# Delta-rule attention and two MLPs on one core: own staging tiles for two chunks, retuned planner numbers, fused masks and GpSimd copies

## The chip, the cores and the metric

The kernel runs on one core of a Trainium2 chip. The metric is the device time of one execution in microseconds, the median of several runs. The engines are named as in the profile: PE is TensorE's matmul side and PEld its weight loads, DVE is VectorE, ACT ScalarE, POOL GpSimd, SP the engine that issues every DMA of this kernel.

## What is computed

```python
def _attn_ref(q, k, v, beta):                      # q, k, v: [4, 8, 768, 48] float32
    k_n = k / (np.linalg.norm(k, axis=-1, keepdims=True) + 1e-06)
    state = np.zeros((B, H, D, D), dtype=np.float32)
    for t in range(S):
        kt, vt, bt = (k_n[:, :, t], v[:, :, t], beta[:, :, t, None])
        y[:, :, t] = np.einsum('bhd,bhde->bhe', q[:, :, t], state)
        v_old = np.einsum('bhde,bhd->bhe', state, kt)
        state = state + bt[:, :, :, None] * np.einsum('bhd,bhe->bhde', kt, vt - v_old)
    return y

# reference: attention, then x = [3072, 384], then two MLPs 384 -> 2048 -> 384
h = x @ w_in;  g = 0 if h <= -1, h if h >= 1, else (h + 1) ** 2 / 4;  x = g @ w_out
h = x @ w_in2; g = h * clip(h + 3, 0, 6) / 6;                         out = g @ w_out2
```

The weights arrive as 64-bit floating-point numbers; the kernel reads their two 32-bit words and makes from them a high and a low fp32r half.

## The kernel before

**Attention.** The 768 steps are cut into 12 chunks of 64. For all 32 heads of a chunk the kernel loads k, v and q, takes the norms of k, and forms, for each half `hb` of the heads, the products of k with k (they go to X, scaled) and of k with q (they go to KQ, and everything past the diagonal is masked to zero). `load_tok` brings the k or q of one half into one of two staging tiles, ST_78 (k) and ST_79 (q), 128x512 each; `transposes` turns the tile on PE into a bank and ACT or DVE copies the bank into KQ; `products` multiplies. Then `inverse` inverts a unit triangular matrix per head, `scale_v` scales v, `wstage` (from chunk 1 on) multiplies the inverse (in G_74 for even chunks, G_75 for odd ones) with k, and `chain` passes the state on and makes y. The y of half 1 of a chunk goes partly through a small tile YS and six DMAs into the MLP's input XB.

**Inverse.** Chunk 0 does its 16 elimination steps on DVE, small instructions of some 0.2 us that each need the one before; chunks 1 to 11 do theirs on POOL.

**MLPs.** Layer 1 takes chunk 0 as a block of 256 columns, chunk 1 as another, then pairs of chunks as blocks of 512; layer 2 takes six blocks of 512. A block goes through 16 slices f of the hidden width: H multiplies XB with WLA or WLB in three steps (high by high, low by high, high by low), ACT and DVE apply the activation and split it into GH and GL, O multiplies these with w_out. For a block of 256 columns H and O of one f are 6 passes of 3 matmuls each, 128x256. `wload` loads one f of the weights raw into one of four RAWL buffers or RAWR and converts it in two halves; each half costs ACT and DVE three or so instructions each (lines 366, 826, 828, 831, 357).

**Order.** No engine's order is written by hand. `Plan` collects the operations with their dependences and a priority; `Plan.emit` places them one by one, always the one that could start soonest by its own table of durations, ties by priority, and what it chooses becomes the in-order queue of each engine. PR holds the priorities (kv, tok, norm, pm, sv, w, chain, y, lv) and its other numbers (a bias for POOL and ACT where an operation could go to several engines, a margin for MLP work). Before the first MLP matmul, wherever PE would idle by the table, `emit` puts filler matmuls `bank_100<-GH_69`, 128x512, whose result nobody reads.

Names used below: `emit`'s filler rule (213 and 427 in its body), `cpalt` (a copy on ACT or DVE, `AD`), `ttalt` (an elementwise operation on DVE or POOL, `DP`), `masking` (the separate mask operation, L535), L506 (X out of the bank), L514 (KQ out of the bank on ACT, mask later) and L516 (the same on DVE, mask at once), L471 (transposes), L389 (all other matmuls).

## Time and profile before

| | us |
|---|---|
| median of 3 runs | 1086.45 |
| lowest and highest run | 1084.42, 1089.5 |
| the profiled execution | 1090.76 |
| its span in the trace | 1089.0 |
| busy PE / DVE / ACT / POOL | 1045.1 / 662.6 / 595.7 / 277.6 |
| first matmul of the MLPs, from the span's start | 87.06 |

The profile is one execution, so times within the span are told as microseconds from its start. PE is busy 96% of the span, but its busy time before 87.06 us holds 176 filler matmuls. The granted clock in the rows (PEclk) is 1.00 for TensorE's upper level of 2.4 GHz; in stretches with parts at 1.2 GHz the mean lies between.

### The profile page before, as it was taken

To read this page: it belongs to the slowest core of one execution; us is meant where nothing else is said; L and a number is where in the kernel's file an instruction comes from. 1 tells how busy PE (TensorE), PEld (TensorE's weight loads), DVE (VectorE), ACT (ScalarE), POOL (GpSimd) and SP (SyncE) were. 2 spreads that over 40 slices of the span, in tenths; PEclk is the share of its full clock that TensorE was granted. 3 is DMA by queue.
4 is the path that set the end of the run, shared out by engine and by line. 5 is a ranking of instruction groups with operands and counts; after the bars stand their busy time and mean duration, and the time that the engine had idled before them with its cause. 6 is when DMAs were issued, how large, how long until landed. Compare 5 with 4: busy or idle time off the path is not lost.

```text
span 1089.0 us, 25916 instructions
## 1 busy us (share of the span) xinstructions
PE 1045.1 (96%) x10684; PEld 890.1 (82%) x10684; DVE 662.6 (61%) x1258; ACT 595.7 (55%) x1164; POOL 277.6 (25%) x652
## 2 busy tenths in 40 slices
...
GB/s 179 191 142 66 61 99 66 45 63 36 59 21 97 69 17 59 90 45 46 40 57 83 80 257 139 116 1 88 1 41 47 1 87 2 59 29 1 29 1 29
DMA packets 174757, 71.86 MB, mean 66 GB/s; under 512 B 121264, under 2 KB 170544, under 8 KB 174640
## 3 DMA queue, kind: packets, MB, share of 16 engines
...
q8 instruction: 84, 1.38, 0.6%
...
## 4 chain that ended last, share of the span: by engine, by line
PE 72%; DVE 11%; ACT 5%; DMA 4%; POOL 3%; issue 3%; SPq 1%; DVEq 0%; POOLq 0%; ACTq 0%
PE bank L389 71%; DMA RAWL<-in_moe_w_in_dram 2%; DVE X L506 2%; POOL TL L571 1%; POOL TMP L566 1%; ACT KQ L514 1%; DVE GF L880 1%; PE bank L471 1%; DVE KQ L535 1%; DMA RAWR<-in_moe_w_in_dram 1%; DVE GL L357 1%; DVE DL L624 1%; ACT G L366 1%; SPq L815 1%; DVE XB L777 1%
## 5 line engine op out<-in xcount | busy, mean ns | idle before, releaser
L389 PE MATMUL bank<-XB,WLA 128*128 128x512 f32 (+1 forms) x1404 | 341.2, 386 | 13.4 <-DMA XB<-YS 7.1
L389 PEld LDWEIGHTS bank<-XB,WLA 128*128 128x128 f32 x1404 | 251.9, 193 | 62.1 <-ACT TBS L828 6.6
L357 DVE TENSOR_TENSOR GL<-GF,GH 128x512 fp32r<-128x512 f32 (+1 forms) x208 | 139.4, 671 | 82.9 <-PE bank L389 57.4
L884 DVE SCALAR_TENSOR_TENSOR GF<-GF,bank 128x512 f32<-128x512 f32 x96 | 66.1, 688 | 193.0 <-ACT GF L883 192.9
L366 ACT ACTIVATE GH<-GF 128x512 fp32r<-128x512 f32 (+1 forms) x202 | 120.9, 599 | 114.3 <-DVE GF L884 69.1
L883 ACT ACTIVATE GF<-bank 128x512 f32<-128x512 f32 x96 | 57.5, 599 | 204.5 <-PE bank L389 203.6
L566 POOL TENSOR_TENSOR TMP<-TL,DL 128x126 f32<-128x126 f32 (+25 forms) x293 | 113.0, 386 | 115.8 <-DVE DL L624 65.7
L571 POOL TENSOR_TENSOR TL<-TL,TMP 128x126 f32<-128x126 f32 (+25 forms) x293 | 126.6, 432 | 23.0
L389 PE MATMUL bank<-GH,WLA 128*128 128x512 f32 (+1 forms) x504 | 121.5, 373 | 2.6 <-DVE GH L368 1.5
L389 PE MATMUL bank<-XB,WLB 128*128 128x512 f32 (+1 forms) x468 | 112.4, 382 | 0.2 <-DVE GF L880 0.2
L389 PE MATMUL bank<-WLA,GH 128*128 128x384 f32 x576 | 112.3, 336 | 0.0
L389 PEld LDWEIGHTS bank<-WLA,GH 128*128 128x128 f32 x576 | 102.8, 188 | 6.4
L389 PEld LDWEIGHTS bank<-GH,WLA 128*128 128x128 f32 x504 | 85.9, 192 | 20.7 <-ACT GH L366 3.5
L389 PEld LDWEIGHTS bank<-XB,WLB 128*128 128x128 f32 x468 | 83.4, 191 | 15.5 <-DVE GF L880 0.4
L880 DVE SCALAR_TENSOR_TENSOR GF<-bank,GF 128x512 f32<-128x512 f32 (+1 forms) x112 | 68.6, 612 | 45.0 <-ACT GF L879 43.8
L878 ACT ACTIVATE GF<-bank 128x512 f32<-128x512 f32 (+1 forms) x112 | 59.8, 534 | 60.6 <-PE bank L389 56.1
L389 PE MATMUL bank<-GL,WLA 128*128 128x512 f32 (+1 forms) x252 | 65.9, 370 | 0.0
L879 ACT ACTIVATE GF<-GF 128x512 f32<-128x512 f32 (+1 forms) x112 | 63.5, 567 | 2.4
L389 PE MATMUL bank<-WLA,GL 128*128 128x384 f32 x288 | 61.5, 334 | 0.0
L389 PEld LDWEIGHTS bank<-WLA,GL 128*128 128x128 f32 x288 | 51.0, 188 | 0.0
L389 PE MATMUL bank<-GH 128*128 128x512 f32 x176 | 50.8, 437 | 0.0
L389 PEld LDWEIGHTS bank<-GL,WLA 128*128 128x128 f32 x252 | 43.9, 191 | 8.2 <-issue 0.3
(135 smaller groups left out, 1357.6 us busy)
## 6 DMA issues: line engine op xcount, KB each, us to landing
...
```

Source lines behind the costliest of these rows:

```text
L357: alts[e] = (d, lambda e=e: ENG[e].tensor_tensor(out=val(out), in0=val(in0), in1=val(in1), op=op))
L366: lambda: nc.scalar.activation(out=val(out), in_=val(in_), func=AF.Copy, scale=scale))
L389: nc.tensor.matmul(o, l, r, start=start, stop=stop)
L471: nc.tensor.transpose(bk.tile[0:112, p * 128:(p + 1) * 128], ST[i][:, p, 0:112], IDN)
L506: P.op("dve", 335, lambda bk=bk, u0=u0, rr=rr, ro=ro: nc.vector.tensor_tensor(out=X[rr, u0:u0 + NP, :], in0=bk.tile[ro].rearrange("p (a x) ...
L566: P.op(te, d, lambda t=t, s=s, r0=r0, a0=a0, a1=a1, m=m: ve.tensor_tensor(out=t[:, a0:a1], in0=TL[:, r0 + a0:r0 + a1, s:s + 1].to_broadcas ...
L571: P.op(te, d, lambda t=t, s=s, r0=r0, a0=a0, a1=a1: ve.tensor_tensor(out=TL[:, r0 + a0:r0 + a1, 0:s], in0=TL[:, r0 + a0:r0 + a1, 0:s], in1 ...
L878: P.op("act", da, lambda: nc.scalar.activation(out=gf, in_=ps, func=AF.Relu, scale=0.5, bias=0.5), r=[hkey(hb)], w=[gk], prio=MP)
L879: P.op("act", da + 48, lambda: nc.scalar.activation(out=gf, in_=gf, func=AF.Square), w=[gk], r=[gk], prio=MP)
L880: P.op("dve", 1.06 * n + 60, lambda: nc.vector.scalar_tensor_tensor(out=gf, in0=ps, scalar=1.0, in1=gf, op0=ALU.max, op1=ALU.min), r=[hkey ...
L883: P.op("act", da, lambda: nc.scalar.activation(out=gf, in_=ps, func=AF.Relu, scale=1.0 / 6.0, bias=0.5), r=[hkey(hb)], w=[gk], prio=MP)
L884: P.op("dve", 1.06 * n + 60, lambda: nc.vector.scalar_tensor_tensor(out=gf, in0=gf, scalar=1.0, in1=ps, op0=ALU.min, op1=ALU.mult), r=[hke ...
```

## The change

PR gets other numbers (kv, tok, norm, pm, sv, w, chain, y, lv, bias, biasa, margin) and new ones (fgap, me, c3, back, dh, and POOL in dw). Beyond that:

- **Staging.** Half 1 of chunks 0 and 1 gets staging tiles of its own: four 128x512 views of G_74 (k and q of chunk 0) and G_75 (chunk 1), zeroed by four more POOL memsets at the start. The zeroing of G itself moves behind the products of its chunk (`zero_g`).
- **Transfers.** A DMA's duration in the planner's table has other values, given per kind; DMAs marked `bulk` (v, weights, tokens and k of chunks 1 and up) are not placed further than `back` ahead of the modelled queue.
- **Masks.** ACT's evacuation of KQ is weighed with 500 more (`extra`), so that DVE's, which masks at once (L516, now L529), is chosen more often and the separate mask less.
- **Copies.** `cpalt` may use POOL for the SBUF to SBUF copies in X, LT and G (`PR["c3"]`), and POOL may do the low-half subtraction of the weights (`dw`).
- **Fillers.** They count 228 or 430 instead of 213 or 427, and must leave 150 instead of 100.
- `wload` takes a list of slices, which holds one everywhere; its views are written in three dimensions.

```diff
+PR = dict(kv=-2.522, tok=-1.749, norm=-2.601, tr=-1.803, prod=-3.087, pm=-0.932, inv=-2.162, sv=0.06, w=-1.449, chain=-0.205, y=-0.76,
+          wl=-0.036, wls=0.003, mp=0, lv=-1.0, first=3.58, bias=83.342, fill=3000, ..., biasa=652.767,
+          ..., fgap=150, me=500, c3=('act', 'dve', 'pool'), back=1500, dh=0, margin=738.749, ..., dw=('dve', 'pool'), pq=190)
...
+                    if o["bulk"]:
+                        t = max(t, dma_free - PR["back"])
...
-                        end = t + o["alts"][e][0] + bias.get(e, 0.0)
+                        ex = o["extra"]
+                        end = t + o["alts"][e][0] + bias.get(e, 0.0) + ex.get(e, 0.0)
...
-                    if x + d > t - 100.0:
+                    if x + d > t - PR["fgap"]:
...
+            if e == "pool":
+                alts[e] = (190 + 1.1 * n, lambda: nc.gpsimd.tensor_copy(val(out), val(in_)))
...
+    gs = [G[i].rearrange("p u e s -> p (u e s)") for i in range(2)]
+    extra = [gs[0][:, 0:512], gs[0][:, 512:1024], gs[1][:, 1024:1536], gs[1][:, 1536:2048]]
+    ST += [x.rearrange("p (a x) -> p a x", a=NP) for x in extra]
...
-        i = stage[0] % NST
+        if c < 2:
+            i = (0 if hb == 0 else 2 + 2 * c) + stage[0] % 2
+        else:
+            i = stage[0] % NST
...
-                                      q=qd(SH[dl], PO[g][dl], SH[dl]))
+                                      q=qd(SH[dl], PO[g][dl], SH[dl]), extra={"act": PR["me"]})
...
-            cpalt(AD, 256, X[p0:p0 + 32, us, 0:32], X[p0:p0 + 32, us, 32:64], False,
+            cpalt(PR["c3"], 256, X[p0:p0 + 32, us, 0:32], X[p0:p0 + 32, us, 32:64], False,
...
+    def zero_g(s_):
+        P.tag = ""
+        zk = [("zg", s_)] + [("gw", s_, hb, dl) for hb in range(2) for dl in range(2)] + tkeys(s_, 0) + tkeys(s_, 1) + \
+            [("st", 2 + 2 * s_ + i, b) for i in range(2) for b in range(2)]
+        zero(G[s_][32:64, :, 0, :], zk, 1200)
+        zero(G[s_][32:64, :, 1, 0:32], zk, 600)
+        zero(G[s_][96:128, :, 0, 0:32], zk, 600)
...
+    for i in range(4):
+        zero(ST[2 + i], [("st", 2 + i)] + ([("braw", 0), ("braw", 1)] if i >= 2 else []), 470)
```

What this makes of the queues, at three places. In the rows a name such as `bank_100` is a bank of PSUM, and `x25` counts equal instructions in a row; a source line is shifted by the change (L471 becomes L484, L389 becomes L396).

**1. PE and SP at the start.** PE, from the last products of half 0 of chunk 0 (`bank_97<-KQ`) to the first of half 1 (`bank_101<-KQ`), before:

```order
L389 MATMUL bank_97<-KQ 64x128 x2
L389 MATMUL bank_100<-GH_69 128x512 x25
L471 MATMUL bank_98<-IDN,ST_78 112x128 x4
L389 MATMUL bank_100<-GH_69 128x512 x3
L471 MATMUL bank_99<-IDN,ST_79 112x128 x4
L389 MATMUL bank_100<-GH_69 128x512 x6
L389 MATMUL bank_101<-KQ 64x128 x2
```

and now:

```order
L396 MATMUL bank_97<-KQ 64x128 x2
L484 MATMUL bank_98<-IDN,G_74 112x128 x4
L484 MATMUL bank_99<-IDN,G_74 112x128 x4
L396 MATMUL bank_100<-GH_69 128x512 x12
L396 MATMUL bank_101<-KQ 64x128 x2
```

34 fillers between the two products have become 12, and both transposes stand right behind the products of half 0. Ahead of the products of half 0 stood 6 fillers, the transposes of k, 2 fillers, those of q, 6 fillers; now 4, k, q, 3.

SP, from the loads of v of chunk 0 on (E_71 is v, KN_77 is k of chunk 1 in natural order, RAWL the raw weights), before:

```order
L429 DMA E_71<-in_v_dram 64x16x48 x2
L422 DMA KN_77<-in_k_dram 64x16x48 x2
L815 DMA RAWL<-in_moe_w_in_dram 48x3x256
L815 DMA RAWL<-in_moe_w_in_dram 16x3x256
L815 DMA RAWL<-in_moe_w_in_dram 48x3x256
L815 DMA RAWL<-in_moe_w_in_dram 16x3x256
L411 DMA ST_78<-in_k_dram 64x8x48 x2
L411 DMA ST_79<-in_q_dram 64x8x48 x2
L815 DMA RAWL<-in_moe_w_out_dram 128x768
```

and now:

```order
L442 DMA E_71<-in_v_dram 64x16x48
L424 DMA G_74<-in_k_dram 64x8x48 x2
L424 DMA G_74<-in_q_dram 64x8x48 x2
L442 DMA E_71<-in_v_dram 64x16x48
L435 DMA KN_77<-in_k_dram 64x16x48 x2
L424 DMA ST_78<-in_k_dram 64x8x48 x2
L424 DMA ST_79<-in_q_dram 64x8x48 x2
L424 DMA G_75<-in_k_dram 64x8x48 x2
L424 DMA G_75<-in_q_dram 64x8x48 x2
L831 DMA RAWL<-in_moe_w_in_dram 48x3x256
```

All tokens of chunks 0 and 1 now go out ahead of the first weights, half 1 of chunk 0 ahead of half of v; before, its loads waited for the staging tiles and stood behind four loads of weights.

**2. POOL beside the inverse of chunk 0**, which runs on DVE. Before, from the last zeroing of G_75 to the first work on chunk 1's inverse (TL):

```order
L399 MEMSET G_74 32x16x32
L399 MEMSET G_75 32x16x64
L399 MEMSET G_75 32x16x32 x2
L357 ISA
L357 TENSOR_TENSOR E_72<-E_72,NRM_90 64x16x48
L574 MEMSET TL 128x512
```

and now, from the zeroing of the new staging views:

```order
L409 MEMSET G_75 128x512 x2
L362 ISA
L362 TENSOR_TENSOR E_71<-E_71,NRM_89 64x16x48
L409 MEMSET G_74 32x16x64
L409 MEMSET G_74 32x16x32 x2
L409 MEMSET G_75 32x16x64
L409 MEMSET G_75 32x16x32 x2
L548 TENSOR_TENSOR KQ<-KQ,MSK 64x4x64 x2
L362 TENSOR_TENSOR E_72<-E_72,NRM_90 64x16x48
L587 MEMSET TL 128x512
```

Half of the scaling of chunk 0's v (E_71), the zeroing of both G and two masks of chunk 1 now stand between the staging's memsets and the scaling of chunk 1's v (E_72).

**3. PE in the first block of the MLP.** Around the transposes of half 1 of chunk 2 (`IDN,ST_78`; `XB,WLA` are passes of H, `GH,WLA` and `GL,WLA` of O; `NH,LT` and `DL,NH` are parts of chunk 1's inverse), before:

```order
L389 MATMUL bank_98<-GL_67,WLA 128x256
L389 MATMUL bank_99<-XB_64,WLA 128x256 x3
L471 MATMUL bank_102<-IDN,ST_78 112x128 x4
L389 MATMUL bank_103<-DL,NH 32x32 x32
L389 MATMUL bank_96<-GH_70,WLA 128x256
```

and now:

```order
L396 MATMUL bank_99<-XB_64,WLA 128x256 x6
L484 MATMUL bank_101<-IDN,ST_78 112x128 x4
L396 MATMUL bank_96<-GH_70,WLA 128x256
...
L396 MATMUL bank_98<-GL_68,WLA 128x256
L396 MATMUL bank_100<-XB_64,WLA 128x256 x9
L396 MATMUL bank_102<-NH,LT 32x32 x32
```

18 matmuls of the MLP now stand between these transposes and the next part of chunk 1's inverse, where there was none. From the first matmul of the MLP to the first of chunk 1's `wstage` (`bank_101<-G_75,KN_77` in both) there were 60 of them and are 108; from the chain of chunk 2 on the two orders hold the same counts of MLP work ahead of each chain, within 8 passes of three.

Over the whole program the fillers go from 176 to 135, DVE's fused mask evacuations (L516) from 7 to 26, its masks of 64x512 from 35 to 22 and of 64x256 from 3 to 9, POOL's of 64x256 from 2 to 9 and of 64x512 from 7 to 4; POOL gets 14 copies, and DVE's instructions go from 1261 to 1245.

## Rows read from the trace of the kernel before

**Rows 1.** Windows: stretch, us, busy PE, PEld, DVE, ACT, POOL (instructions), clock, DMA, GB/s.

```profile
28.26:62.00 33.74, 29.80 (x417) 22.80 (x419) 31.10 (x89) 27.27 (x57) 3.33 (x3) 1.00 0.91 194
...
87.06:121.00 33.94, 24.92 (x520) 21.56 (x520) 28.41 (x69) 27.37 (x59) 2.49 (x4) 0.72 0.31 68
121.00:177.00 56.00, 52.87 (x1038) 49.02 (x1039) 45.44 (x104) 42.79 (x101) 13.23 (x39) 0.94 0.30 62
177.00:640.00 463.00, 452.68 (x5995) 367.55 (x5996) 344.01 (x627) 303.77 (x599) 239.40 (x556) 1.00 0.29 64
```

**Rows 2.** Waits of PE, whole span: us in total, times, longest.

```profile
PE bank L389 <- DMA XB<-YS: 7.1, 2, 6.4
```

**Rows 3.** Timeline of PE, 8 to 27 us: start, us, instruction, count, idle before and releaser.

```profile
10.95 1.05 PE L471 MATMUL bank<-IDN,ST 128*112 128x128 f32 x4
...
14.32 1.10 PE L389 MATMUL bank<-KQ 48*64 48x128 f32 x32
15.35 5.97 PE L389 MATMUL bank<-GH 128*128 128x512 f32 x25
...
24.22 1.10 PE L389 MATMUL bank<-KQ 48*64 48x128 f32 x32
```

**Rows 4.** Timeline of ACT, 10 to 29 us.

```profile
15.46 1.17 ACT L514 ACTIVATE KQ<-bank 64x256 f32<-64x256 f32 x3 [2.14 <-PE bank L389]
...
22.93 1.21 ACT L366 ACTIVATE KQ<-bank 48x512 f32<-48x512 f32 x2 [0.48 <-PE bank L471]
```

**Rows 5.** Timeline of SP's queue, 4 to 14 us.

```profile
8.85 2.15 SPq L422 DMA_DIRECT2D KN<-in_k_dram  x2
11.05 2.40 SPq L815 DMA_DIRECT2D RAWL<-in_moe_w_in_dram  x4
```

**Rows 6.** Tile view, 0 to 60 us: landing of ST, then of RAWL.

```profile
DMA to landing us min/median/max: 3.1/4.0/5.9
...
DMA to landing us min/median/max: 3.6/4.4/6.8
```

**Rows 7.** Timeline of DVE, 20 to 62 us.

```profile
27.00 0.36 DVE L826 TENSOR_SCALAR TBS<-RAWL 128x384 int32<-128x384 int32 x1
29.57 1.10 DVE L587 STREAM_TRANSPOSE DL<-X 128x512 f32<-128x512 f32 x1
...
44.22 0.21 DVE L571 TENSOR_TENSOR TL<-TL,TMP 128x60 f32<-128x60 f32 x1
44.35 1.63 DVE L826 TENSOR_SCALAR TBS<-RAWL 128x384 int32<-128x384 int32 x1
...
55.61 0.71 DVE L605 STREAM_TRANSPOSE NH<-DL 128x512 f32<-128x512 f32 x1
```

**Rows 8.** Timeline of POOL, 40 to 60 us.

```profile
43.10 2.67 POOL L357 TENSOR_TENSOR E<-E,NRM 64x768 f32<-64x768 f32 x1 [32.92 <-DVE X L506]
```

**Rows 9.** Groups by form, whole span: busy us, mean ns of one, idle before.

```profile
L535 POOL TENSOR_TENSOR KQ<-KQ,MSK 64x256 f32<-64x256 f32 x2 | 1.5, 728 | 25.5 <-ACT KQ L514 25.5
...
L535 DVE TENSOR_TENSOR KQ<-KQ,MSK 64x512 f32<-64x512 f32 x35 | 24.2, 690 | 1.8 <-ACT KQ L514 1.3
...
L516 DVE TENSOR_TENSOR KQ<-bank,MSK 64x256 f32<-64x256 f32 x7 | 3.0, 423 | 1.1 <-ACT KQ L514 1.0
...
L357 DVE TENSOR_TENSOR E<-E,NRM 64x768 f32<-64x768 f32 x21 | 20.2, 961 | 0.4
```

**Rows 10.** Timeline of PE, 55 to 96 us.

```profile
61.13 1.39 PE L389 MATMUL bank<-DL,NH 32*32 32x32 f32 x116 [1.77 <-issue]
...
71.44 0.31 PE L389 MATMUL bank<-DL,NH 32*32 32x32 f32 x6 [1.39 <-issue]
...
87.06 1.16 PE L389 MATMUL bank<-XB,WLA 128*128 128x256 f32 x2 [6.45 <-DMA XB<-YS]
88.92 3.75 PE L389 MATMUL bank<-XB,WLA 128*128 128x256 f32 x16 [0.70 <-DMA XB<-YS]
```

**Rows 11.** Groups by form of DVE, 87.06 to 121 us.

```profile
L826 DVE TENSOR_SCALAR TBS<-RAWR 128x384 int32<-128x384 int32 x4 | 1.3, 334 | 3.2 <-DMA RAWR<-in_moe_w_in_dram 3.2
```

More of the change, by code (lines that the diff above doesn't have):

```diff
@@ L47, in __init__, with op @@
         self.tag = ""
-    def op(self, eng, dur, fn, r=(), w=(), prio=0.0, pre=(), alloc=(), uses=(), nbytes=0, own=(), crit=False, alts=None, dyn=None, load=0.5, port=(), tiled=False, q=(0, 0, 0), urgent=False):
+    def op(self, eng, dur, fn, r=(), w=(), prio=0.0, pre=(), alloc=(), uses=(), nbytes=0, own=(), crit=False, alts=None, dyn=None, load=0.5, port=(), tiled=False, q=(0, 0, 0), urgent=False, bulk=False, extra=None):
         i = len(self.ops)
@@ L76, in dma @@
         kw.setdefault("prio", 0.0)
-        return self.op("sp", 475 + (175 if ndesc >= 512 else 0), fn, nbytes=nbytes * max(1.0, 512.0 / run), **kw)
+        cost = kw.pop("cost", None) or nbytes * max(1.0, 400.0 / run) / 360.0
+        return self.op("sp", 475 + (200 if ndesc >= 512 else 0), fn, nbytes=cost * 360.0, **kw)
     def emit(self, banks, spare, fill):
@@ L175, in emit @@
                         cand = k
-                if cand is not None and HOLD and e == "dve":
-                    lim = cand[0] + HOLD
+                if cand is not None and PR["dh"] and e == "dve":
+                    lim = cand[0] + PR["dh"]
                     end = cand[0] + ops[cand[3]]["alts"][e][0]
@@ L371, in cpalt @@
                            lambda: nc.vector.tensor_scalar(out=val(out), in0=val(in_), scalar1=scale, scalar2=None, op0=ALU.mult))
-        return P.op(None, 0, None, alts=alts, port=() if ps else ("dve",), **kw)
+        return P.op(None, 0, None, alts=alts, port=() if ps else ("dve", "pool"), **kw)
     AD = PR["ad"]
@@ new lines, in wload @@
+            P.dma(lambda o=o, a=a: nc.sync.dma_start(out=o, in_=a), rows * KT, rows * 1024 * KT * (nf if i < len(parts) - 1 else KT),
+                  w=[rkey + (i,)], pre=[rkey], prio=prio, bulk=perm,
+                  cost={48: 620.0, 16: 310.0}.get(rows))
+        v3 = lambda ap: ap.rearrange("p (a c) -> p a c", a=KT)
+        for k, f in enumerate(fs):
+            P.tag = f"wl f{f} {perm}"
+            for pc in range(2):
+                n = wcount[0]
+                wcount[0] += 1
+                tk, sk = ("tb", n % 2), ("sx", n % 2)
+                tb, s_ = tmps[n % 2]
+                sl = (DM * pc, DM * pc + DM)
+                if pc == 0:
+                    hl = ri[:, :, 256 * k:256 * k + 256].rearrange("p a (c t) -> p t a c", t=2)
+                else:
+                    hl = ro[:, k, :].rearrange("p (a c t) -> p t a c", a=KT, t=2)
+                lw, hw = hl[:, 0], hl[:, 1]
+                need = [rkey] + [rkey + (i,) for i in (range(len(parts) - 1) if pc == 0 else [len(parts) - 1])]
+                cpalt(AD, DM, v3(tb.bitcast(F32)), hw.bitcast(F32), False, 2.0 ** -112, r=need, w=[tk], prio=prio)
+                P.op("dve", 67 + 0.53 * DM, lambda s_=s_, hw=hw: V.tensor_scalar(
+                    out=v3(s_), in0=hw, scalar1=-2147483648, scalar2=None, op0=ALU.bitwise_and), r=need, w=[sk], prio=prio, port=("dve",))
+                P.op("act", 495, lambda s_=s_, lw=lw: nc.scalar.activation(
+                    out=s_.bitcast(I16).rearrange("p (a c t) -> p t a c", a=KT, t=2)[:, 0], in_=lw.bitcast(U32), func=AF.Relu, scale=0.875 * 2.0 ** -29, bias=0.49),
+                    r=need + [sk], w=[sk], prio=prio)
+                P.op("dve", 466, lambda tb=tb, s_=s_: V.scalar_tensor_tensor(
+                    out=tb, in0=tb, scalar=3, in1=s_, op0=ALU.logical_shift_left, op1=ALU.bitwise_or),
+                    r=[tk, sk], w=[tk], prio=prio, port=("dve",))
+                cpalt(AD, DM, lambda f=f, sl=sl: wl(f, 0, *sl), tb.bitcast(F32), False, r=[tk, ("wlb", f >= NFA)], w=[("w", f, pc, 0)], prio=prio)
+                ttalt(DW, DM, lambda f=f, sl=sl: wl(f, 1, *sl), tb.bitcast(F32), lambda f=f, sl=sl: wl(f, 0, *sl).bitcast(F32), ALU.subtract,
+                      r=[tk, ("w", f, pc, 0)], w=[("w", f, pc, 1)], prio=prio)
@@ L944, in load2 @@
                     out=XB[xi][:, j, hl, :].bitcast(F32).rearrange("p (b s) -> p b s", b=B), in_=s_), 128 * B, 128 * 512 * 4,
-                    r=[("x2", c, j, hl) for c in cs], w=[("x2b", xi, j, hl)], pre=allx, prio=20)
+                    r=[("x2", c, j, hl) for c in cs], w=[("x2b", xi, j, hl)], pre=allx, prio=20, cost=870.0)
     def fin2(bi, cs):
```

77 lines of the change are left out of this document (27 added, 50 removed).

## The prediction, made before the changed kernel was run

> **What bounds the kernel now.** I read the windows first [rows 1]. From 177 to 640 us PE is busy 452.68 of 463 us, from 121 to 177 us 52.87 of 56: there only PE's own work counts, and an engine beside it may gain or lose a few microseconds unseen. The start is another matter. PE's busy time before 87.06 us is filled up with dummy matmuls, and the first matmul of the MLPs starts at 87.06 behind a wait for the shipment of y [rows 2, 10]; nothing can saturate PE before that. From 28.26 to 62 us DVE is busy 31.10 of 33.74: the elimination steps of chunk 0's inverse share it with weight conversion, masks and scaling. From 87.06 to 121 us PE idles 33.94 - 24.92 = 9.0 us, at a mean granted clock of 0.72, parts of it at 1.2 GHz, while DVE is busy 28.41 and ACT 27.37: those two set this stretch. So I follow one path: loads and products of chunk 0, its inverse on DVE, the tail (PE and evacuations) to the first MLP matmul, then the stretch behind it. What is gained at its end stays to the end if PE has the same work ahead of it; the orders of PE say so from the chain of chunk 2 on.
>
> **Part 1: products of chunk 0.** Before, the products of half 0 start at 14.32, behind the transposes of q at 10.95, which stood behind 2 fillers [rows 3]. Those 2 fillers are gone and 3 instead of 6 follow; I take 0.9 us off (13.4); the transposes ahead could give less, and not above 1.7, since ACT's two evacuations of q, 1.21 us, stay [rows 4]. Half 1: its products start at 24.22, 9.90 us after those of half 0, of which 25 fillers take 5.97 us, 0.239 each [rows 3]; 34 have become 12. What then sets the distance is ACT, in order: the evacuations of half 0's KQ (three take 1.17 us, a fourth 0.39), X copies, k, and q's two, 1.21 us [rows 4], with PE's products (1.10) ahead of them. With the X copies at 0.4 each like the KQ evacuations, and k at half of q's two, I count 1.1 + 1.6 + 0.8 + 0.6 + 1.2 = 5.3 and take 5.5, which 12 fillers (2.9 us) and two sets of transposes fit into. Are the data there? The four DMAs into G_74 are issued from about 8.1 us, half a load of v behind 7.4, to about 10.7, by SP's pace of 1.1 us for a DMA of this size (8.85, 2.15 for two) [rows 5]; with a landing of 4.0, at most 5.9 [rows 6], they are in by 14.7, one of them by 16.6 at worst, about when PE gets to them (14.5). So products of half 1 at 18.9 instead of 24.22: **-5.3**, from -4.5 to -6.1.
>
> **Part 2: from the products to the inverse.** Before, 29.57 - 24.22 = 5.35 us pass [rows 3, 7], with a weight conversion of 0.36 at 27.00 and others on DVE and ACT between the evacuations. At 18.9 the weights are not yet converted: SP issued them from 11.05 us [rows 5] and now does from about 18.6, behind twelve token loads, landing 4.4 later [rows 6]. That frees DVE for the evacuations: **-0.6** (0 to -0.8).
>
> **Part 3: the inverse on DVE**, 55.61 - 29.57 = 26.04 us [rows 7], busy almost throughout. The order has 77 instructions on DVE between these two both before and after. One scaling (0.961), two masks (0.690 each) go, two fused evacuations (0.423 each) and a weight conversion (0.35) come [rows 7, 9]: 0.96 + 1.38 - 0.85 - 0.35 = -1.14 us. Against it stands POOL: two masks of 0.73 each [rows 9] and six zeroings. In the trace, while POOL scaled v for 2.67 us from 43.10 [rows 8], DVE's elimination steps kept their 0.21, but a weight conversion took 1.63 instead of 0.36, 1.27 more [rows 7]. By that row's ratio, 1.27 of 2.67, the masks' 1.46 us hold DVE for 0.7; if a one-input instruction falls under each, up to 1.4; the zeroings, which no row shows beside DVE, between nothing and as much as the masks. The weights, landing from about 23, could be late by up to 1 us for a DVE that starts the inverse at 23.6. Net **0**, from -1.1 to +2.3.
> The Trainium skill (SBUF — State Buffer, "two separate sides") says that VectorE and GpSimd share a port pair as an exclusive lock, held for the whole instruction, against a VectorE instruction with two SBUF inputs too. By it the masks alone would cost their full 1.46 us, this part +0.3 and the time 1078.3. The trace agrees for the conversion, and not for the two-input steps, which ran at 0.21 beside the scaling; no run here shows a POOL copy beside DVE.
>
> **Part 4: the tail**, 87.06 - 55.61 = 31.45 us [rows 7, 10]. PE's order in it is the same but for the fillers, so **0**. PE twice waited for nothing that the trace names, 1.77 and 1.39 us [rows 10]; if these don't come back, -3.2; other fillers behind the inverse, some at 1.2 GHz, +1.7.
>
> So the first MLP matmul starts at 87.06 - 5.3 - 0.6 = 81.2.
>
> **Part 5: from there to 177 us.** 48 more MLP matmuls stand ahead of chunk 1's `wstage`, 108 for 60, though from chunk 2's chain on the counts agree. One costs 3.75 / 16 = 0.234 at 1.2 GHz [rows 10], half of that, 0.117, at 2.4: 5.6 us of work moved into a stretch with 9.0 us idle. What they can fill is what DVE and ACT feed: DVE has 33.94 - 28.41 = 5.5 us free there, and needs part of it for their activations. One wait does go: DVE stood 3.2 us for RAWR [rows 11], ahead of the products and the inverse of chunk 2, and that weight slice no longer stands ahead of them. I take **-2.5**, nearest to that row; from 0 (the place of the wait is taken by another) to -6 (all 48 fill idle time).
>
> **Part 6: the rest.** From 177 us on the masks and copies that move from DVE to POOL, or from ACT to DVE's fused form (19 evacuations more at 0.423, 13 masks less at 0.690 [rows 9]), are hidden under PE, with 10.3 us idle left in 463 [rows 1]: **0**, plus or minus 3, since a POOL queue that now holds copies beside the elimination steps of chunks 1 to 11 could make an inverse late, and one mask less could make it early. Layer 2 does not change.
>
> **Sum.** -5.3 - 0.6 + 0 + 0 - 2.5 + 0 = -8.4 us. On the profiled execution, 1090.76, that is 1082.4; that execution is 4.3 above the median of 1086.45, and the gain is a difference, so the prediction is 1086.45 - 8.4 = **1078.0**.
>
> **Rivals.** *Given back* (1082 to 1086, taken as 1084): the first MLP matmul comes 5.9 us sooner, but the stretch from there to 121 us is set by DVE and ACT, busy 28.41 and 27.37 of 33.94 [rows 1], and their work doesn't move sooner with it: weights now come later, and by the order each of the two has three conversions fewer behind it when the chain of chunk 0 ends, some 1.5 us. Then all or most of the 5.9 becomes PE's idle time. For it: these engines' load. Against it: 9 us idle and DVE's wait of 3.2. The change would have done what it says at the start and brought nothing.
> *The MLP ahead of the attention* (slower): PE works in order, and the 8 more slices f (6 passes each) stand ahead of chunk 1's `wstage`, on which chains 1, 2 and so on wait. In the stretch before, 60 matmuls, 10 such units, took 33.4 us, 3.3 each, since each waits for the activations of the one before; at PE's own pace one takes 0.7. If the units are paced by DVE and ACT, each costs above 0.7 what the path of the attention loses: with part 5's gain gone, 1080.5 + 8 x (p - 0.7), which passes 1086.45 + 5.4 from p = 2.1 on; at 2.3 it is 1093, at 3.3 1101. Against it: the work is needed anyway and idle time of the stretch takes most of it.
> *More* (1068 to 1073): with the RAWR wait gone and 48 more matmuls PE's 9.0 us idle and its half-speed parts mostly vanish, -5.6 or more in part 5, and the two unnamed waits of part 4 don't return.
>
> **How the numbers follow.** Forecast 0.58 (1074 to 1081), given back 0.24, slower 0.08, more 0.10. The range of 8 in 10 is 1069 to 1086: the forecast, nearly all of "given back" and most of "more". Half a per cent, 5.4 us, is about what a measurement of this kernel can tell from no change: faster than 1081.0 are the forecast and "more", 0.68; within it "given back", 0.24; slower 0.08.
>
> **What would show it.** In the profile after: products of half 1 at 18 to 19.5 us (part 1), the first transpose of the inverse at 23 to 24.5 (2), its last at 49 to 51 (3), the first MLP matmul at 80 to 83 (4), PE's idle time in the 34 us after that under 7 (5), and from 177 us on the same idle as before within 3 (6). Part 1 is wrong if PE waits for the DMAs into G_74; part 3 if DVE rows stretch beside POOL's masks or wait for RAWL; part 5 if chunk 1's `wstage`, which closes the stretch to 121 us, has not come forward by 5 us or more.

## The result, and the profile after

| | before | after |
|---|---|---|
| median of the runs beside each other (4 each) | 1087.45 | 1076.84 |
| lowest and highest | 1084.42, 1089.5 | 1076.25, 1078.28 |
| profiled execution, its span | 1090.76, 1089.0 | 1078.28, 1076.5 |
| first MLP matmul | 87.06 | 80.26 |
| filler matmuls | 176 | 135 |

The ratio is 0.9897, 95% interval 0.9872 to 0.9921: about 11 us faster, where 1078.0 was forecast. The windows of the changed kernel, cut at the events of the prediction (inverse's first transpose, about the end of its steps, first MLP matmul, chunk 1's `wstage`, the chain of chunk 2), answer to [rows 1]:

```profile
core 0: us, PE busy (x) PEld busy (x) DVE busy (x) ACT busy (x) POOL busy (x), PEclk, DMA share, GB/s
14.00:26.04 12.04, 12.04 (x104) 9.97 (x97) 6.30 (x16) 6.67 (x15) 3.40 (x4) 1.00 1.05 188
26.04:51.00 24.96, 22.45 (x154) 17.75 (x153) 23.87 (x78) 19.26 (x40) 5.63 (x6) 1.00 0.98 218
...
80.26:116.42 36.16, 28.08 (x565) 25.46 (x565) 32.65 (x79) 31.91 (x71) 4.04 (x9) 0.75 0.39 87
116.42:165.80 49.38, 45.94 (x992) 42.19 (x991) 41.87 (x94) 37.50 (x89) 15.20 (x38) 0.97 0.35 71
165.80:1076.50 910.70, 894.99 (x8194) 762.60 (x8193) 521.05 (x920) 469.67 (x895) 244.65 (x572) 1.00 0.23 56
```

Behind the first MLP matmul DVE and ACT are still the busiest (32.65 and 31.91 of 36.16 us), and PE still idles 8.1 us there. From the first MLP matmul to chunk 1's `wstage` the timelines count 108 MLP matmuls, and 60 before. DVE's conversions from RAWR, which waited 3.2 us before [rows 11], wait no more there:

```profile
L850 DVE TENSOR_SCALAR TBS<-RAWR 128x384 int32<-128x384 int32 x4 | 1.4, 354 | 0.0
```

The timeline of PE in the changed kernel, which answers to [rows 3, 10]:

```profile
12.93 2.59 PE L396 MATMUL bank<-KQ 48*64 48x128 f32 x32 [0.17 <-ACT KQ L373]
15.46 1.95 PE L484 MATMUL bank<-IDN,G 128*112 128x128 f32 x8
17.06 4.40 PE L396 MATMUL bank<-GH 128*128 128x512 f32 x12
21.39 1.10 PE L396 MATMUL bank<-KQ 48*64 48x128 f32 x32
...
57.66 1.19 PE L396 MATMUL bank<-DL,NH 32*32 32x32 f32 x73 [1.45 <-issue]
...
80.26 0.55 PE L396 MATMUL bank<-XB,WLA 128*128 128x256 f32 x1 [7.11 <-DMA XB<-YS]
82.20 4.37 PE L396 MATMUL bank<-XB,WLA 128*128 128x256 f32 x17 [1.39 <-DMA XB<-YS]
```

The order is the one forecast (both transposes right behind the products, 12 fillers, products of half 1), but the products of half 0 took 2.59 us and not 1.10, and the fillers 0.37 each and not 0.24. That is PE at half pace up to about 19.9 us. The clock column does not show it: it reads 1.00 from 14.00 to 26.04. In the kernel before, fillers at 62.45 take 0.45 each where the column reads 0.50:

```profile
62.45 3.17 PE L389 MATMUL bank<-GH 128*128 128x512 f32 x7
```

```profile
62.50:65.00 2.50, 2.50 (x7) 2.02 (x7) 2.44 (x5) 1.69 (x3) 0.00 (x0) 0.50 0.76 216
```

So where this text puts PE at 1.2 or 2.4 GHz in the first 20 us, it goes by this pace, and the clock as its cause is inferred.

In the timelines of DVE, and below it of POOL, the inverse runs from 26.04 to 51.69:

```profile
26.04 1.08 DVE L600 STREAM_TRANSPOSE DL<-X 128x512 f32<-128x512 f32 x1
...
38.43 0.57 DVE L584 TENSOR_TENSOR TL<-TL,TMP 128x64 f32<-128x64 f32 x1
...
39.48 0.75 DVE L579 TENSOR_TENSOR TMP<-TL,DL 128x63 f32<-128x63 f32 x1
...
51.69 0.71 DVE L618 STREAM_TRANSPOSE NH<-DL 128x512 f32<-128x512 f32 x1
```

```profile
15.20 1.47 POOL L362 TENSOR_TENSOR E<-E,NRM 64x768 f32<-64x768 f32 x1 [7.02 <-DMA E<-in_v_dram]
...
38.18 1.97 POOL L548 TENSOR_TENSOR KQ<-KQ,MSK 64x256 f32<-64x256 f32 x2 [4.40 <-issue]
40.69 1.56 POOL L362 TENSOR_TENSOR E<-E,NRM 64x768 f32<-64x768 f32 x1 [0.55 <-DMA E<-in_v_dram]
```

Two elimination steps, 0.21 before [rows 7], take 0.57 and 0.75 while POOL masks. And ACT at the start:

```profile
10.27 0.60 ACT L373 ACTIVATE KQ<-bank 112x512 f32<-112x512 f32 x1 [7.62 <-PE bank L484]
10.89 1.28 ACT L459 ACT_TABLE_LOAD   x1
12.18 0.21 ACT L459 ACTIVATE SM<-SM 128x16 f32<-128x16 f32 x1
12.30 1.19 ACT L373 ACTIVATE KQ<-bank 48x512 f32<-48x512 f32 x2
```

A table load of 1.28 us stands in the path of the norms and of q's evacuation. Before, the norms' Sqrt was queued ahead of k's evacuation, and the load ran at 2.67 us while ACT was idle.

Between equal events the span of 1089.0 lost 12.5 us: up to the products of half 1, 24.22 to 21.39, -2.8; to the inverse, 5.35 to 4.65, -0.7; the inverse, 26.04 to 25.65, -0.4; the tail, 31.45 to 28.57, -2.9; and from the first MLP matmul to the end, 1001.94 to 996.24, -5.7.

### The profile page after: what moved, and what is told of

The parts are those of the page before. It is cut to its first block, busy times and chain, and to the rows that moved or that the text cites. A ratio compares the mean times of both kernels' runs of the same rounds, so it can differ in the third digit from the quotient of the medians.

```text
span 1076.5 us, 25827 instructions
## 1 busy us (share of the span) xinstructions
PE 1030.6 (96%) x10643; PEld 879.5 (82%) x10643; DVE 652.9 (61%) x1242; ACT 591.4 (55%) x1156; POOL 291.8 (27%) x677
## 4 chain that ended last, share of the span: by engine, by line
PE 58%; DVE 6%; ACT 4%; POOL 2%; issue 1%; DMA 1%; DVEq 0%; ACTq 0%; POOLq 0%
PE bank L396 58%; POOL TMP L579 1%; POOL TL L584 1%; DVE GF L904 1%; ACT GH L373 1%; ACT G L373 1%; DVE XB L790 1%; DVE X L519 1%; DVE DL L637 1%; DMA KN<-in_k_dram 1%; PE bank L484 0%; DVE DL L645 0%; ACT GF L903 0%; ACT GF L902 0%; ACT NH L373 0%
## 5 line engine op out<-in xcount | busy, mean ns | idle before, releaser
L396 PE MATMUL bank<-XB,WLA 128*128 128x512 f32 (+1 forms) x1404 | 338.1, 383 | 13.0 <-DMA XB<-YS 8.5
L396 PEld LDWEIGHTS bank<-XB,WLA 128*128 128x128 f32 x1404 | 249.7, 191 | 61.6 <-ACT TBS L852 7.2
L362 DVE TENSOR_TENSOR GL<-GF,GH 128x512 fp32r<-128x512 f32 (+1 forms) x208 | 137.0, 660 | 87.0 <-PE bank L396 59.4
L579 POOL TENSOR_TENSOR TMP<-TL,DL 128x126 f32<-128x126 f32 (+25 forms) x293 | 115.2, 393 | 89.3 <-DVE DL L637 46.0
L584 POOL TENSOR_TENSOR TL<-TL,TMP 128x126 f32<-128x126 f32 (+25 forms) x293 | 121.5, 415 | 22.9
L396 PE MATMUL bank<-GH,WLA 128*128 128x512 f32 (+1 forms) x504 | 121.5, 373 | 0.8 <-ACT GH L373 0.5
L396 PE MATMUL bank<-XB,WLB 128*128 128x512 f32 (+1 forms) x468 | 112.6, 381 | 0.2 <-DVE GF L904 0.2
L396 PE MATMUL bank<-WLA,GH 128*128 128x384 f32 x576 | 112.3, 336 | 0.0
L396 PEld LDWEIGHTS bank<-WLA,GH 128*128 128x128 f32 x576 | 102.8, 188 | 6.4
L396 PEld LDWEIGHTS bank<-GH,WLA 128*128 128x128 f32 x504 | 86.1, 193 | 17.8 <-ACT GH L373 2.4
L396 PEld LDWEIGHTS bank<-XB,WLB 128*128 128x128 f32 x468 | 83.4, 190 | 15.8 <-DVE GF L904 0.4
L396 PE MATMUL bank<-GL,WLA 128*128 128x512 f32 (+1 forms) x252 | 66.3, 372 | 2.0 <-DVE GL L362 1.9
L396 PE MATMUL bank<-WLA,GL 128*128 128x384 f32 x288 | 61.5, 334 | 0.0
L396 PEld LDWEIGHTS bank<-GL,WLA 128*128 128x128 f32 x252 | 44.3, 193 | 10.8 <-DVE GL L362 3.0
L396 PEld LDWEIGHTS bank<-WLA,GL 128*128 128x128 f32 x288 | 51.0, 188 | 0.0
L373 ACT ACTIVATE KQ<-bank 48x512 f32<-48x512 f32 (+1 forms) x69 | 40.7, 589 | 9.8 <-PE bank L484 8.6
```

What stands on the lines that cost most here:

```text
L362: alts[e] = (d, lambda e=e: ENG[e].tensor_tensor(out=val(out), in0=val(in0), in1=val(in1), op=op))
L373: lambda: nc.scalar.activation(out=val(out), in_=val(in_), func=AF.Copy, scale=scale))
L396: nc.tensor.matmul(o, l, r, start=start, stop=stop)
L579: P.op(te, d, lambda t=t, s=s, r0=r0, a0=a0, a1=a1, m=m: ve.tensor_tensor(out=t[:, a0:a1], in0=TL[:, r0 + a0:r0 + a1, s:s + 1].to_broadcas ...
L584: P.op(te, d, lambda t=t, s=s, r0=r0, a0=a0, a1=a1: ve.tensor_tensor(out=TL[:, r0 + a0:r0 + a1, 0:s], in0=TL[:, r0 + a0:r0 + a1, 0:s], in1 ...
```

## The experiments

Three things are compared for each run: the time of the first MLP matmul; PE's idle time in the 130 us behind it; and the mean granted clock there. Three of these windows, of the kernel before, of the changed one, and of the one with the staging alone:

```profile
87.06:217.06 130.00, 114.91 (x2432) 105.05 (x2433) 105.28 (x240) 97.22 (x224) 25.51 (x73) 0.89 0.31 65
```

```profile
80.26:210.26 130.00, 115.03 (x2517) 105.73 (x2518) 109.42 (x247) 102.39 (x235) 35.06 (x95) 0.92 0.35 72
```

```profile
83.01:213.01 130.00, 110.94 (x2377) 101.34 (x2378) 105.97 (x240) 95.78 (x220) 27.66 (x80) 0.84 0.33 70
```

A clock of 0.89 is 22% of the window at 1.2 GHz, which loses half of that, 0.11 x 130 = 14.3 us. The table has these for all runs; the last column is span - first MLP - idle - lost to the clock. Idle time at 1.2 GHz counts twice in this, as idle and as lost, so the last column comes out low where both are large.

| kernel | median | ratio to before (interval) | products half 1 | first MLP | idle in 130 | clock | span | rest |
|---|---|---|---|---|---|---|---|---|
| before | 1087.45 | | 24.22 | 87.06 | 15.1 | 0.89 | 1089.0 | 972.5 |
| changed | 1076.84 | 0.9897 (0.9872 to 0.9921) | 21.39 | 80.26 | 15.0 | 0.92 | 1076.5 | 970.8 |
| staging taken back | 1084.69 | 0.9959 (0.9942 to 0.9976) | 19.45 | 80.42 | 19.5 | 0.88 | 1082.7 | 967.2 |
| staging alone | 1095.48 | 1.0062 (1.0043 to 1.0081) | 20.16 | 83.01 | 19.1 | 0.84 | 1093.2 | 970.3 |
| old transfer costs | 1074.06 | 0.9859 (0.9835 to 0.9884) | 19.38 | 79.45 | 11.0 | 0.93 | 1072.2 | 972.7 |
| no fused preference | 1087.40 | 0.9985 (0.9968 to 1.0002) | 20.99 | 83.97 | 19.1 | 0.92 | 1086.2 | 972.7 |
| old numbers | 1085.34 | 0.9964 (0.9943 to 0.9986) | 18.97 | 77.46 | 18.5 | 0.85 | 1082.7 | 967.3 |
| no POOL copies | 1080.65 | 0.9923 (0.9893 to 0.9952) | 21.18 | 81.68 | 17.9 | 0.91 | 1079.8 | 968.5 |
| MLP held back | 1082.41 | 0.9933 (0.9911 to 0.9955) | 20.98 | 81.63 | 16.8 | 0.90 | 1078.6 | 967.2 |
| fillers in the wait | 1077.72 | 0.9886 (0.9862 to 0.9910) | 20.38 | 81.69 | 15.8 | 0.95 | 1076.4 | 972.4 |
| early table load | 1079.07 | 0.9883 (0.9859 to 0.9907) | 17.88 | 81.37 | 15.4 | 0.92 | 1078.0 | 970.8 |
| masks on DVE | 1077.55 | 0.9874 (0.9847 to 0.9901) | 20.80 | 81.91 | 15.2 | 0.94 | 1077.3 | 972.4 |
| old costs, fillers in the wait | 1074.62 | 0.9847 (0.9824 to 0.9870) | 18.81 | 80.12 | 10.1 | 0.93 | 1071.4 | 972.1 |
| three fillers more (one run) | 1080.53 | | 18.87 | 79.81 | 15.3 | 0.91 | 1078.7 | 971.9 |

The kernel before took 1088.4, 1091.5 and 1090.06 us beside the three sets of runs, so ratios are the safer comparison. The rest stays within 967 to 973 while the spans go from 1071 to 1093.

Where in the 130 us PE idles differs too. These are the parts from chunk 1's `wstage` on, of the kernel before, of the changed one, of the one with the staging alone, and of the one with the old transfer costs:

```profile
120.51:217.06 96.55, 90.31 (x1916) 83.66 (x1917) 76.97 (x172) 70.20 (x166) 23.02 (x69) 0.95 0.31 64
```

```profile
116.42:210.26 93.84, 86.95 (x1954) 80.27 (x1954) 76.77 (x169) 70.47 (x165) 31.02 (x86) 0.98 0.34 66
```

```profile
114.51:213.01 98.50, 84.74 (x1853) 78.11 (x1853) 77.16 (x170) 67.18 (x158) 25.20 (x76) 0.91 0.34 65
```

```profile
108.47:209.45 100.98, 96.01 (x2118) 88.70 (x2119) 83.92 (x186) 76.86 (x179) 35.54 (x100) 1.00 0.33 68
```

Idle behind `wstage` is 6.2, 6.9, 13.8 and 5.0 us in these four; ahead of it, in all runs, 5.3 to 9.3.

**Staging taken back.** All but the own staging tiles (and the later zeroing of G) as changed.

```diff
...
-        if c < 2:
-            i = (0 if hb == 0 else 2 + 2 * c) + stage[0] % 2
-        else:
-            i = stage[0] % NST
+        i = stage[0] % NST
...
```

> The changed kernel with its own staging taken back (half 1 of chunks 0 and 1 goes through the two shared staging tiles again, G is zeroed at the start), everything else as changed. Theory A (the own staging is what brings the start forward): the loads of half 1 wait again for the transposes of half 0 (10.2 to 11.5 us), so the products of half 1 of chunk 0 come at 23 to 24.5 us instead of 21.4, the first MLP matmul 2 to 3 us later than 80.3, and the time is 1079 to 1081. Rival B (the retuned order brings it: loads of half 1 no longer behind four weight loads, fewer fillers): products of half 1 within 1 us of 21.4, time 1075 to 1079.

The products of half 1 came at 19.45, 1.9 us earlier than with the staging, and the first MLP matmul at 80.42, equal to the changed kernel's 80.26. The loads of half 1 did go out behind the transposes of half 0, at 10.58 and 12.00 us, but still ahead of the weights, and that was early enough: theory A's 23 to 24.5 us did not come. The 1.9 us are mostly PE's pace, which rose earlier here. Where it rose early with the staging in place and the table load late as here (old numbers, three fillers more, below), the products came at 18.97 and 18.87, so the tiles are worth about 0.5 us at this point. Rival B was nearer on the start and wrong on the time, 1084.69. The loss lies later; PE in this kernel waits, 98 to 113 us behind its first MLP matmul,

```profile
181.09 1.28 PE L396 MATMUL bank<-NH,LT 32*32 32x32 f32 x128 [2.62 <-DVE NH L612]
...
189.89 0.68 PE L478 MATMUL bank<-IDN,ST 128*112 128x128 f32 x4 [1.98 <-DVE DL L627]
193.40 1.92 PE L396 MATMUL bank<-NH,LT 32*32 32x32 f32 x64 [1.54 <-ACT KQ L373]
```

for parts of chunk 3's inverse. The changed kernel reaches the first of them at 182.50 and does not wait: it has 378 MLP matmuls behind it by then, this one 351. These tiles serve chunks 0 and 1 only, so I put the difference down to the order that the planner made; no run separates the two.

**Staging alone**, on the kernel before (with the zeroing of G moved).

```diff
...
+        if c < 2:
+            i = (0 if hb == 0 else 2 + 2 * c) + stage[0] % 2
+        else:
+            i = stage[0] % NST
-        i = stage[0] % NST
...
```

> The kernel before with the own staging alone (and the zeroing of G moved), numbers and planner as before. Theory A: products of half 1 of chunk 0 at 19 to 22 us instead of 24.2, first MLP matmul 3 to 5 us earlier than 87.1, time 1082 to 1084. Rival B: the start comes forward likewise, but the stretch behind the first MLP matmul gives it back, 1085 to 1089; the gain of the whole change is then in the retuned order of that stretch.

The start does come forward, products of half 1 at 20.16 and the first MLP matmul at 83.01, as theory A had it. The time is above both expectations: the 130 us behind it idle 4.0 us more than before and lose 6.5 us more to the clock. A start that is 4 us earlier ended in a run 0.6% slower. `wstage` still came 6.0 us earlier, 114.51 for 120.51, with 69 MLP matmuls ahead of it for 60; the loss lies behind it (13.8 us idle for 6.2), not where rival B put it.

**Old transfer costs**, and bulk transfers not held back.

```diff
-        cost = kw.pop("cost", None) or nbytes * max(1.0, 400.0 / run) / 360.0
-        return self.op("sp", 475 + (200 if ndesc >= 512 else 0), fn, nbytes=cost * 360.0, **kw)
+        kw.pop("cost", None)
+        return self.op("sp", 475 + (175 if ndesc >= 512 else 0), fn, nbytes=nbytes * max(1.0, 512.0 / run), **kw)
...
-                    if o["bulk"]:
-                        t = max(t, dma_free - PR["back"])
```

> The changed kernel with the planner's old transfer costs and without the holding back of bulk transfers. Its SP queue still has all tokens of chunks 0 and 1 ahead of the first weights. Theory A (staging and start): time within 2 us of 1077. Rival C (the transfer times decide when weights arrive and with them the stretch behind the first MLP matmul): DVE or ACT wait for RAWL or RAWR by 2 us or more in all in that stretch, and the time is 1080 or more.

Neither: 1074.06, the change without this part is no slower, and with its ratio of 0.9859 beside 0.9897 (intervals overlap) probably a little faster. The gain is in idle time, 11.0 for 15.0. The table load is early again here, since its order has the Sqrt first.

**No preference for fused masks.**

```diff
-          ..., fgap=150, me=500, ...
+          ..., fgap=150, me=0, ...
```

> The changed kernel without the preference for the fused mask (the 500 ahead of ACT's evacuation becomes 0), so DVE does more separate masks of 0.69 and fewer fused evacuations of 0.42. Theory A (masks are hidden under PE from 177 us on and cost 1 us at most before): within 2 us of 1077. Rival D (DVE and ACT set the stretch from 80 to 116 us, so DVE's load counts in full): 1080 or more.

The time is rival D's, 1087.40, no gain left; not for D's reason, since its stretch from the first MLP matmul to `wstage` is shorter (31.2 us for 36.2, with 63 MLP matmuls in it for 108) and `wstage` comes at 115.15, 1.3 us earlier. Part of the loss lies ahead of that stretch, in the tail, 34.12 us for 28.57, here with DVE and ACT busy 26.16 and 26.63 us; the rest lies behind `wstage`, where PE idles 11.5 us for 6.9. The tail:

```profile
49.85:83.97 34.12, 17.98 (x599) 14.85 (x597) 26.16 (x56) 26.63 (x54) 13.11 (x36) 0.79 0.68 156
```

The same stretch of the changed kernel has 22.63 and 21.00:

```profile
51.69:80.26 28.57, 19.21 (x610) 16.00 (x610) 22.63 (x51) 21.00 (x42) 11.29 (x32) 0.84 0.65 142
```

**Fillers in the wait**: 26 more on PE where it waits 7.11 us for the shipment of y.

The edit, in short:

```diff
+        a = first PE operation of H, layer 1, block 0, f 0
+        order[a:a] = 26 fillers
```

> The changed kernel with 26 more fillers on PE, between the last matmul of chunk 0's y and the first of the MLPs, where PE waits 7.1 us for the shipment of y; no other queue changes. Theory K (the clock pays for PE's idle time: the trace of the changed kernel shows 1.2 GHz from 78.1 to 95.2 us, right behind that wait): the granted clock stays at 2.4 GHz through most of the stretch behind the first MLP matmul, PE's matmuls there take half the time, and the time falls by 3 to 7 us, to 1070 to 1074. Rival L (DVE and ACT set that stretch, busy 32.65 and 31.91 of 36.16 us): the clock rises, PE idles more between, and the time stays within 1.5 us of 1077.

Rival L. The clock in the 130 us rises to 0.95, 3.9 us less lost, and nothing comes of it in the time. The first MLP matmul is 1.4 us later, which need not be the fillers': a wait of PE in the tail that the trace does not explain is 3.78 us in this execution and 1.45 in the changed kernel's. From the first MLP matmul to `wstage` the kernel needs 36.07 us with DVE busy 32.55 and ACT 31.88, as before the fillers:

```profile
81.69:117.76 36.07, 27.43 (x565) 25.18 (x565) 32.55 (x79) 31.88 (x71) 3.80 (x8) 0.81 0.37 88
```

DVE and ACT set this stretch; from `wstage` to the end it is 1.4 us faster, which makes up for the later first matmul. Such fillers, 28 of them at the same place, on the kernel with the old transfer costs:

> The kernel with the old transfer costs (1074.1) with 28 more fillers in the wait ahead of the first MLP matmul, 7.84 us there; its clock is at 1.2 GHz from 76.4 to 83.3 and from 90.1 to 103.7 us. Theory K: 3 to 6 us less, 1068 to 1071. Rival L: within 1.5 us of 1074.

Rival L again, 1074.62 for 1074.06.

**Early table load**: a Sqrt of 16 zeros on ACT at the start.

```diff
+    P.op("act", 200, lambda: nc.scalar.activation(out=SM[:, 9, :], in_=GF[0][:, 0:U], func=AF.Sqrt), r=[("gf", 0)], w=["sm9"], prio=-29)
```

> The changed kernel with one small Sqrt of 16 columns on ACT right at the start, so that ACT's table load of 1.28 us, which stands at 10.9 us ahead of the norms' Sqrt and of q's evacuation, falls into idle time at 2.7 us. Theory M (the late table load cost part 1 of the prediction): q's evacuation and the norms come 1.3 us earlier or more, the products of half 0 at 11.5 to 12.2 us instead of 12.9, those of half 1 at 19.7 to 20.7 instead of 21.4, the first MLP matmul about 1 us earlier. Rival K (PE's clock: the first products take 2.59 us at 1.2 GHz instead of 1.10, the 12 fillers 4.40 instead of 2.9): the products of half 0 start earlier, but those of half 1 stay within 0.5 us of 21.4.

PE's timeline of this kernel:

```profile
12.80 1.25 PE L396 MATMUL bank<-KQ 48*64 48x128 f32 x32
...
17.88 0.43 PE L396 MATMUL bank<-KQ 48*64 48x128 f32 x2
```

The load moved to 2.68 us. The products of half 0 came only 0.13 us earlier, 12.80 for 12.93, since PE's fillers ahead of them end no sooner; theory M had 11.5 to 12.2. Those of half 1 came 3.5 us earlier, more than M's 0.7 to 1.7. About 1.0 of that is the load: with the load late and PE at full pace from the products on, they come at 18.97 (old numbers) and 18.87 (three fillers more), for 17.88 here. The other 2.5 are PE's pace, which in this run was that of 2.4 GHz from the products on. The inverse began 2.9 us earlier, and the first MLP matmul did not: the tail took 31.62 us, its clock 0.78 (0.84 in the changed kernel). The time is the same.

**Three fillers more** ahead of the first transposes. The edit, in short:

```diff
+        a = first PE operation of the transposes of chunk 0, half 0, k
+        order[a:a] = 3 fillers
```

> The changed kernel with 3 more fillers ahead of the first transposes, where PE waits 1.69 us for k; no other queue changes. In three runs with the changed kernel's queues at the start PE's first rise from 1.2 to 2.4 GHz, by the spacing of its fillers (0.43 against 0.23 us), came at 17.3, 18.8 and 19.9 us; before it came at about 14 us, with 14 fillers ahead of the products of half 0 instead of 7. Theory K (more work ahead brings the rise): at 16 us or earlier, products of half 1 at 20.0 or earlier. Rival V (chance or something else sets it): between 17 and 20 us as in the three runs.

PE's timeline of this kernel, from the last three fillers ahead of the products of half 0 on:

```profile
10.92 0.94 PE L401 MATMUL bank<-GH 128*128 128x512 f32 x3
12.89 0.43 PE L401 MATMUL bank<-KQ 48*64 48x128 f32 x2 [1.02 <-ACT KQ L378]
...
15.38 3.01 PE L401 MATMUL bank<-GH 128*128 128x512 f32 x12
18.87 0.43 PE L401 MATMUL bank<-KQ 48*64 48x128 f32 x2 [0.49 <-ACT KQ L378]
```

The fillers at 10.92 already take 0.31 each, and the products of half 1 come at 18.87, as theory K has it, in a single run. Two other runs with 7 fillers there (early table load, old numbers) rose by 13 us as well, so it is not shown that the fillers did it. The gain of 2.5 us was 0.45 at the first MLP matmul, and none at the end.

**Masks on DVE**: the two masks of chunk 1, half 1. The edit, in short:

```diff
+        for o in masks of chunk 1, half 1, that stand on POOL:
+            o["eng"], o["fn"] = "dve", o["alts"]["dve"][1]
```

> The changed kernel with the two masks of chunk 1, half 1, at the same place in the order but on DVE instead of POOL. In the changed kernel they run on POOL from 38.18 for 1.97 us, and two of DVE's elimination steps beside them take 0.57 and 0.75 instead of 0.21. Theory P (POOL's instruction holds DVE's two-input steps): these steps fall back to 0.21 to 0.23, 0.9 us gained, against two masks of 0.42 more on DVE, so the inverse ends within 0.4 us of where it did and the time is within 2 us of 1077. Rival Q (the steps are longer for another reason): they stay at 0.5 or more, and the inverse ends 0.8 us later.

Theory P. Both steps are back at 0.21 (the first is shown); a later one waits instead for the scaling of v, which now starts beside it (DVE, then POOL):

```profile
37.83 0.21 DVE L588 TENSOR_TENSOR TL<-TL,TMP 128x64 f32<-128x64 f32 x1
...
42.04 1.45 DVE L588 TENSOR_TENSOR TL<-TL,TMP 128x60 f32<-128x60 f32 x1
```

```profile
41.94 1.48 POOL L366 TENSOR_TENSOR E<-E,NRM 64x768 f32<-64x768 f32 x1 [8.75 <-DMA E<-in_v_dram]
```

It ends where POOL's instruction ends. The inverse took 26.40 us, within what runs with unchanged queues there took (25.65 and 26.46), and the time is the same.

**No POOL copies**, and no weight halves on POOL.

```diff
-          ..., c3=('act', 'dve', 'pool'), ...
+          ..., c3=('act', 'dve'), ...
-          ..., dw=('dve', 'pool'), ...
+          ..., dw=('dve',), ...
```

> The changed kernel with no POOL copies and no weight halves on POOL (ACT and DVE do them, as before). Theory A (they are hidden under PE): within 2 us of 1077. Rival T (they relieve DVE and ACT in the stretch behind the first MLP matmul, where the changed kernel has some 5 of them): DVE or ACT end that stretch later and the time is 1080 or more. Rival U (POOL beside DVE costs more than it relieves): 1075 or less.

1080.65, the ratio 0.9923 with an interval that overlaps the changed kernel's: U is out, A and T are not told apart. Idle time in the 130 us is 2.9 us more.

**MLP held back**: H of the slices from f4 on waits for chunk 1's `wstage` (which now writes the key `wd`).

```diff
...
-            P.op("pe", KT * (n * 0.4515 + 1), pe, r=xkeys + wkeys(f, (0,), wh), w=...
+            P.op("pe", KT * (n * 0.4515 + 1), pe, r=xkeys + wkeys(f, (0,), wh) + ([("wd",)] if blk == 0 and layer == 1 and f >= 4 else []), w=...
```

> The changed kernel with one dependence more in the planner: H of the slices f4 and up of the first block may start only behind chunk 1's wstage, so about 30 of the 48 MLP matmuls that had come ahead of it stand behind it again. Theory R (part 5 of the prediction: they fill idle time and cost the attention little): wstage comes some 3 us earlier, 112 to 114 us, PE idles more there, and the time is 1078 to 1082. Rival S (they stand in the attention's way): wstage and all chains come 3 us earlier, the time is 1072 to 1075.

Nearer to theory R, a little outside both of its ranges: 72 MLP matmuls stand ahead of `wstage` for 108, `wstage` comes at 114.92 for 116.42, and the time is 0.9933 of before, 0.4% or about 4 us above the changed kernel, with intervals that just overlap; idle time is 1.8 us more, and 2.6 us more go to the clock. In this order the MLP's early matmuls are probably worth more than the attention loses by them. Their number alone does not decide: the kernel with the old transfer costs has 57 of them there and is faster.

**Old numbers** with all the new parts.

```diff
-PR = dict(kv=-2.522, tok=-1.749, norm=-2.601, ..., pm=-0.932, ..., sv=0.06, w=-1.449, chain=-0.205, y=-0.76, ...
+PR = dict(kv=-2.451, tok=-1.879, norm=-2.407, ..., pm=-1.495, ..., sv=-0.287, w=-1.124, chain=-0.022, y=-0.474, ...
```

> The changed kernel with the priorities, biases and the margin of the kernel before (kv, tok, norm, pm, sv, w, chain, y, lv, bias, biasa, margin); staging, transfer costs, fused masks and POOL copies as changed. Theory B (the numbers make the order that gains): no gain left or a loss, 1084 to 1095, with a tail and a stretch behind the first MLP matmul like those of the run with the staging alone. Rival A (the new parts make it): 1075 to 1080.

Theory B on the time, 1085.34. It has the earliest first MLP matmul of all runs, 77.46, 9.6 us ahead of before, and gives back 3.5 us in idle time and 9.1 us to the clock against the changed kernel.

## Why the prediction was right, and where it was not

The total held, -8.4 forecast and -10.6 in the medians, and the first MLP matmul came at 80.26 for 81.2. That it did is in part luck: part 1 brought 2.5 us too little, and part 4, which was put at nothing, 2.9. The steps held less well:

- **Part 1, -5.3, measured -2.8.** The distance of 5.5 us between the two products was right where PE ran at 2.4 GHz: 5.08 with the early table load, 5.98 with three more fillers. In the changed kernel's trace it was 8.46. The step took 0.239 for a filler from a stretch at full clock [rows 3], though the change also removes 7 of 14 fillers ahead of it, and by the pace of the fillers PE stayed at 1.2 GHz until about 19.9 us; why it did so in this run and not in others is open. And the step looked at the order of the evacuations on ACT, not at the table load that the new order puts between those of half 0, worth about 1.0 us where PE is fast.
- **Part 2, -0.6, measured -0.7.** Right.
- **Part 3, 0, measured -0.4.** Within its range, with its objection wrong. It held that two-input steps don't wait for POOL, on the strength of steps that kept 0.21 beside one scaling. In the changed kernel steps took 0.57 and 0.75 beside the masks, and 0.21 when the masks were moved. What the Trainium skill (SBUF — State Buffer, "two separate sides") says of two-input instructions is what these traces show; the price by it, the masks' full 1.46 us, was above the 0.9 measured. The row that spoke against it was misread: POOL's scaling of 2.67 us takes 1.47 at 15.20 in the changed kernel, so it probably waited itself for the first 1.2, beside the steps of 0.21, and held DVE only from about 44.3, where the conversion took 1.63.
- **Part 4, 0, measured -2.9.** One of the two unnamed waits came back (1.45), the other did not, and the six fillers ahead of the chain took 1.65 us where seven had taken 3.03 at 1.2 GHz. The wait that came back is 1.45 to 3.78 us in the six runs with this order in the tail, for no reason that a trace names. The part has no fixed length: 27.5 to 34.1 us in the runs here.
- **Part 5, -2.5, measured -5.7 to the end of the span.** The direction held, and moving 36 of the MLP matmuls back cost about 4 us. DVE's wait of 3.2 us for RAWR is gone, as the step said. The 48 matmuls more made the stretch to `wstage` 2.7 us longer (36.16 for 33.45). From there to the end the span lost 8.4 us, and the 48, which no longer have to be done there, are 5.6 of it at the prediction's price. That is 2.9 together, near its 2.5. The other 2.8 it did not have; the mean clock behind `wstage` is 0.98 for 0.95, but as fillers in the wait won 3.9 us by the clock and no time, the cause is not shown. Idle time did not fall as the step has it: 8.1 us in the first 34 where under 7 was named, 15.0 for 15.1 in the 130. `wstage` was to come forward by 5 us or more; it came forward by 4.1.
- **The cause.** The argument that a gain at the start stays to the end was the weak point. It held for the changed kernel; with the staging alone 4.05 us at the first MLP matmul became a loss, with the old numbers 9.6 us became 6.3 of span, with the early table load 2.9 us at the inverse became nothing. What went with the time is PE's idle time behind chunk 1's `wstage`: 3.8 and 5.0 us in the two kernels with the old transfer costs, 6.9 to 7.5 in the changed kernel and the four that leave its order behind the start alone, 8.9 to 13.8 in the six others that change a part. (The kernel before has 6.2 there, and the latest first MLP matmul.) The prediction had taken the stretch from 121 us on for one where only PE's own work counts, by its 52.87 of 56 us; other orders did wait there. The number of MLP matmuls ahead of `wstage` does not go with the time: 57 in the fastest kernel, 60 before, 63 without the fused preference, 108 in the changed kernel and with the staging taken back. These are single profiled executions, and why one order idles more than another is not shown. "Given back", at 0.24, was a better rival than its chance said, though what was given back went behind `wstage` and not in the stretch that it named.

What stays open: which single part of the change earns how much. Each of three undone alone (staging, fused masks, numbers) costs 0.6 to 0.9%, the POOL copies 0.3% with overlapping intervals, and leaving out the new transfer costs loses nothing; but each undoing made the planner write another order for the whole program, and the numbers had been set for the full change. The kernel with the old transfer costs is the fastest here, 0.9859 and, with fillers in the wait, 0.9847.
